# RWKV-6 attention and a SwiGLU feed-forward in one kernel: two casts of v go from ScalarE to VectorE, and products of r and k are placed behind the copies of x^T

## The chip, the core and the metric

The kernel runs on one core of one Trainium2 chip. A core has TensorE (PE) for matmuls, VectorE (DVE), ScalarE (ACT) and GpSimd (POOL) for everything elementwise, and SyncE (SP), which here only issues DMAs. Each engine works through its own queue in order, and semaphores tie the queues together. GpSimd issues the DMAs that cast weights from float32 to bfloat16 on their way, so those stand in its queue between its products. The metric is the device time of one execution in microseconds.

## What is computed

The reference has two parts. The first is a linear attention with a decaying state, for 4 batches, 8 heads, 768 steps and head size 48:

```
cur  = einsum('bhd,bhe->bhde', u * k[t], v[t])
y[t] = einsum('bhd,bhde->bhe', r[t], state + cur)
state = w[t][..., None] * state + einsum('bhd,bhe->bhde', k[t], v[t])
```

The second takes y as x, 3072 rows of 384, through an RMS norm with gain and a gated feed-forward (FFN) of width 1536:

```
xn  = x / sqrt(mean(x * x) + 1e-06) * rms_g
out = (silu(xn @ w_gate) * (xn @ w_val)) @ w_out
```

All inputs and the output are float32.

## The kernel before

**Tiles.** The 768 steps are cut into 6 superblocks of 128 steps. In a superblock the 4 batches give 4 units, so unit n.j is superblock n of batch j, a tile of 128 steps by 384 columns. A step of the program has a name such as k_mul.1.0: the function k_mul for unit 1.0. For the FFN the second number is one of 12 groups of 128 hidden columns, and the 512 rows of a whole superblock are worked at once.

**A unit's way.** load_r, load_k, load_v and load_w (lines 245 to 270) bring its inputs, issued by SP. ln, cs_mm, exp_r and exp_k make the decay factors. r_mul and k_mul (454 to 463) multiply r and k by them on VectorE and write the bfloat16 tile rk; from superblock 2 on, k_mul runs on GpSimd. rk_pe (480) transposes rk on TensorE, rk_tr (486) copies the result out of PSUM on ScalarE; from superblock 2 on a DMA transposes instead. q_mm (495) makes the products of all pairs of steps, q_mask_e and q_mask_o (508, 515) drop those of later steps; in superblock 0 both run on VectorE, later ScalarE copies the odd heads (q_copy_o) and GpSimd masks them. cast_v (376) makes a bfloat16 copy vb of v. y_mm (542) multiplies the masked products by vb and adds the old state's share; st_mm and st_new (523, 533) make the next state, also from vb. The step's own term, with u, goes over GpSimd: bonus_mul (465) is two products, bonus_sum (470) a sum by VectorE, bonus_v (475) a product with v; x_pe (in superblock 0) or x_add adds it. x_sq, x_rstd and xn_mul normalise, xn_pe (592) transposes x on TensorE and xn_out (598) copies x^T with the gain on VectorE.

**The FFN.** gate_mm and val_mm (637, 644) each do 3 matmuls on x^T of all 4 units, silu (651) runs on ScalarE, h_mul (655) on VectorE, and o_mm (668) does 12 matmuls per unit with wo_sb, then o_out and out_dma. The FFN of superblock n runs mixed with the attention of superblock n+1. load_gv.g.h (348) loads gate (h = 0) or value (h = 1) weights, piece 0 for groups 0 to 3 and piece 1 for groups 4 to 11; load_wo (356) loads w_out in three pieces of 4 groups. Both are issued from GpSimd's queue. The steps warm are matmuls on zeros, whose result is not used.

**What sets the order.** ORDER (line 25) is a list of all 1086 steps written out by hand, and the loop at line 691 calls them one after the other. Each engine gets its own steps in the order of the list. PSUM banks are handed out in the same order from three rings: a (2 banks: cs_r, gates, x_pe), b (2 banks: cs_k, values, x_pe) and q (4 banks: all else). A new step takes the bank whose last user comes earliest in the list, and waits for that user. Sets of units, such as CAST_ACT at line 177, choose the engine of a step.

The lines that the change touches in the code are these:

```
    CAST_ACT = sel("00 01 02 03 10 11 12 13")
...
        if (n, j) in CAST_ACT:
            nc.scalar.copy(out=vb[n, j], in_=inp["v", n, j])
        else:
            nc.gpsimd.tensor_copy(out=vb[n, j], in_=inp["v", n, j])
```

Of the kernel before, what the change touches and what calls it, by code (L numbers as in the profile page):

```python
# [41 lines left out]
xn_out.0.1 bonus_mul.1.1 warm.11.0 xn_mul.0.3 exp_k.1.3 xn_out.0.0 st_mm.0.3 xn_out.0.2 st_mm.0.2 xn_pe.0.3 exp_r.1.3
st_new.0.3 cs_mm.1.2 rk_pe.1.0 xn_out.0.3 k_mul.1.1 st_mm.0.1 st_new.0.1 k_mul.1.3 gate_mm.0.0 exp_r.1.2 bonus_sum.1.0
exp_k.1.2 rk_pe.1.1 gate_mm.0.3 rk_tr.1.0 val_mm.0.0 silu.0.0 bonus_sum.1.1 load_gv.1.1 load_r.2.2 bonus_mul.1.3
silu.0.3 val_mm.0.2 rk_tr.1.1 h_mul.0.0 gate_mm.0.2 st_new.0.2 silu.0.2 gate_mm.0.1 bonus_sum.1.3 val_mm.0.3
gate_mm.0.9 silu.0.1 h_mul.0.2 val_mm.0.1 gate_mm.0.6 silu.0.9 r_mul.1.3 h_mul.0.3 q_mm.1.0 h_mul.0.1 silu.0.6
q_mask_e.1.0 q_copy_o.1.0 q_mask_o.1.0 gate_mm.0.11 gate_mm.0.7 q_copy_o.1.1 silu.0.7 rk_pe.1.3 q_mask_e.1.1
q_mask_o.1.1 r_mul.1.2 bonus_v.1.0 val_mm.0.6 val_mm.0.7 cast_v.1.0 k_mul.1.2 rk_tr.1.3 gate_mm.0.5 h_mul.0.6 y_mm.1.0
load_wo.0.0 val_mm.0.9 silu.0.11 bonus_v.1.1 cast_v.1.2 load_wo.1.0 st_mm.1.0 cast_v.1.1 gate_mm.0.4 rk_pe.1.2
h_mul.0.7 st_mm.1.1 silu.0.5 val_mm.0.5 x_add.1.0 rk_tr.1.2 h_mul.0.9 cast_v.1.3 gate_mm.0.10 bonus_mul.1.2 val_mm.0.4  # L50
st_new.1.0 st_new.1.1 load_wo.2.0 q_mm.1.2 h_mul.0.5 silu.0.4 x_sq.1.0 h_mul.0.4 gate_mm.0.8 bonus_v.1.3 q_copy_o.1.3
x_rstd.1.0 q_mask_e.1.3 q_copy_o.1.2 val_mm.0.8 silu.0.8 val_mm.0.11 y_mm.1.1 silu.0.10 q_mask_e.1.2 bonus_sum.1.2
q_mask_o.1.3 h_mul.0.8 x_add.1.1 y_mm.1.3 st_mm.1.2 load_v.2.1 ln.2.0 st_mm.1.3 q_mask_o.1.2 val_mm.0.10 y_mm.1.2
x_sq.1.1 xn_mul.1.0 bonus_v.1.2 cs_mm.2.0 x_add.1.3 x_sq.1.3 st_new.1.2 h_mul.0.11 ln.2.1 h_mul.0.10 x_add.1.2
cs_add.2.0 o_mm.0.0 o_out.0.0 x_rstd.1.1 x_sq.1.2 xn_pe.1.0 xn_out.1.0 xn_mul.1.1 exp_r.2.0 st_new.1.3 cs_mm.2.1
cs_add.2.1 x_rstd.1.2 load_r.2.3 r_mul.2.0 o_mm.0.2 xn_pe.1.1 xn_mul.1.2 xn_pe.1.2 x_rstd.1.3 o_mm.0.1 xn_mul.1.3
bonus_mul.2.0 xn_out.1.1 exp_k.2.0 out_dma.0.0 load_k.2.2 exp_r.2.1 w_tot.2.0 load_v.2.0 ln.2.2 k_mul.2.0 ln.2.3
w_tot.2.1 r_mul.2.1 cs_mm.2.2 xn_pe.1.3 cs_mm.2.3 exp_k.2.1 xn_out.1.2 cs_add.2.2 k_mul.2.1 cs_add.2.3 cast_v.2.1
exp_r.2.2 exp_r.2.3 rk_tr.2.1 xn_out.1.3 o_mm.0.3 exp_k.2.3 o_out.0.1 w_tot.2.2 r_mul.2.2 bonus_mul.2.1 gate_mm.1.7
val_mm.1.7 exp_k.2.2 load_k.2.3 st_mm.2.1 rk_tr.2.0 bonus_sum.2.0 r_mul.2.3 w_tot.2.3 gate_mm.1.1 load_v.2.2 st_new.2.1  # L60
k_mul.2.2 silu.1.7 bonus_mul.2.2 silu.1.1 bonus_sum.2.1 val_mm.1.1 h_mul.1.7 gate_mm.1.6 silu.1.6 bonus_v.2.1
gate_mm.1.5 cast_v.2.0 k_mul.2.3 silu.1.5 rk_tr.2.2 val_mm.1.5 load_w.3.3 o_out.0.2 h_mul.1.1 gate_mm.1.3 gate_mm.1.0
val_mm.1.0 h_mul.1.5 o_out.0.3 silu.1.0 val_mm.1.6 q_mm.2.0 load_v.2.3 q_copy_o.2.0 silu.1.3 q_mask_o.2.0 gate_mm.1.2
st_mm.2.0 h_mul.1.0 val_mm.1.3 rk_tr.2.3 h_mul.1.6 load_w.3.1 load_w.3.0 gate_mm.1.10 val_mm.1.2 load_k.3.1
q_mask_e.2.1 silu.1.2 st_new.2.0 gate_mm.1.4 q_copy_o.2.1 cast_v.2.2 silu.1.4 q_mask_o.2.1 h_mul.1.3 q_mask_e.2.0
y_mm.2.1 y_mm.2.0 h_mul.1.2 st_mm.2.2 bonus_v.2.0 silu.1.10 x_add.2.1 x_add.2.0 gate_mm.1.9 val_mm.1.4 x_sq.2.1
gate_mm.1.8 val_mm.1.9 bonus_mul.2.3 st_new.2.2 out_dma.0.1 x_sq.2.0 h_mul.1.4 load_v.3.2 x_rstd.2.0 silu.1.9 silu.1.8
q_mm.2.2 bonus_sum.2.2 q_copy_o.2.2 h_mul.1.9 gate_mm.1.11 q_copy_o.2.3 out_dma.0.2 load_w.3.2 cast_v.2.3 bonus_v.2.2
bonus_sum.2.3 q_mask_o.2.3 st_mm.2.3 load_k.3.0 q_mask_o.2.2 q_mask_e.2.3 val_mm.1.11 q_mask_e.2.2 val_mm.1.10
bonus_v.2.3 y_mm.2.3 silu.1.11 y_mm.2.2 ln.3.0 h_mul.1.11 h_mul.1.10 x_rstd.2.1 x_add.2.2 ln.3.1 val_mm.1.8 ln.3.3  # L70
h_mul.1.8 cs_mm.3.0 load_r.3.0 x_sq.2.2 xn_mul.2.0 cast_v.3.2 cs_add.3.0 x_add.2.3 exp_k.3.0 x_sq.2.3 o_mm.1.0
cs_mm.3.1 xn_pe.2.0 exp_r.3.0 ln.3.2 x_rstd.2.2 o_mm.1.1 st_new.2.3 load_r.3.1 out_dma.0.3 w_tot.3.0 r_mul.3.0
xn_mul.2.1 k_mul.3.0 xn_mul.2.2 cs_add.3.1 exp_k.3.1 xn_pe.2.2 cs_mm.3.3 x_rstd.2.3 o_out.1.0 exp_r.3.1 bonus_mul.3.1
xn_out.2.2 xn_mul.2.3 o_mm.1.3 w_tot.3.1 xn_pe.2.3 o_out.1.1 cs_add.3.3 r_mul.3.1 load_k.3.2 load_r.3.3 xn_pe.2.1
xn_out.2.0 exp_r.3.3 exp_k.3.3 cs_mm.3.2 xn_out.2.3 o_mm.1.2 load_r.3.2 k_mul.3.1 w_tot.3.3 rk_tr.3.0 r_mul.3.3
cs_add.3.2 out_dma.1.0 xn_out.2.1 load_v.3.0 exp_r.3.2 gate_mm.2.5 exp_k.3.2 r_mul.3.2 w_tot.3.2 val_mm.2.0 gate_mm.2.0
bonus_mul.3.0 bonus_mul.3.2 k_mul.3.2 o_out.1.3 bonus_sum.3.0 silu.2.5 rk_tr.3.1 load_k.3.3 o_out.1.2 q_mm.3.0 silu.2.0
q_mask_e.3.0 val_mm.2.1 bonus_v.3.0 h_mul.2.0 gate_mm.2.1 load_w.4.1 load_v.3.1 load_k.4.3 st_mm.3.2 k_mul.3.3
q_copy_o.3.0 silu.2.1 rk_tr.3.2 load_v.4.0 rk_tr.3.3 val_mm.2.5 gate_mm.2.11 load_k.4.0 bonus_sum.3.1 cast_v.3.0
out_dma.1.1 load_v.3.3 load_w.5.2 q_mask_e.3.1 q_copy_o.3.1 gate_mm.2.2 silu.2.11 h_mul.2.5 val_mm.2.2 h_mul.2.1  # L80
load_w.4.0 gate_mm.2.3 load_v.4.1 silu.2.2 q_mask_o.3.0 cast_v.3.1 load_r.4.1 bonus_sum.3.2 h_mul.2.2 bonus_v.3.1
# [643 lines left out]
```

## Time and profile before

| what | value |
|---|---|
| three runs | 199.61, 200.89 and 200.95 us, median 200.89 |
| span of the profiled execution | 199.4 us |
| TensorE busy | 194.7 us |
| VectorE, ScalarE, GpSimd busy | 151.5, 137.1, 125.7 us |
| first matmul of the FFN (gate_mm.0.0) | 31.30 us from the span's start |
| first matmul with wo_sb (o_mm.0.0) | 52.66 us |

The profiled execution's own time is its span, first to last instruction. A timeline row reads: start, duration, engine, line, operation, output tile and input tiles, shape, count, and in brackets the idle time of that engine just before it with what ended it. Consecutive like instructions are merged, hence the count. In a row of waits stand the total, the number of times and the longest, in us. In a row of DMA issues stand the count, the size of one in KB as written, and the median time from the start of the issue to the landing. In a row for one line or tile stand the shortest, median and longest duration in ns, and the first and last start in us. Rows carry line numbers, not step names. The program's order gives the name: the n-th row of a line on an engine is the n-th step of that function in ORDER. The bank letters in ps_qu, ps_av and so on are the rings with one letter per bank (u, v, x, z).

### The profile page before, as it was taken

The numbers are of one execution on the slowest core, as the hardware profiler recorded it, in microseconds if no ns is written. First come the engines' busy times: TensorE is split into PE (matmuls) and PEld (weight loads), VectorE is DVE, ScalarE is ACT, GpSimd is POOL, SyncE is SP. The second block draws the span as 40 slices with busy tenths as digits, with TensorE's granted clock in tenths as the row PEclk, the third lists the DMA queues.
The fourth block names the chain that finished last, engine by engine and source line by source line (L and its number), as shares of the span: only waits on it lengthen the run. The fifth ranks groups of instructions, "written<-read, shape, count | busy, mean of one in ns | idle before, by whom it ended". The sixth has DMA issues, their size and how long they took to land.

```text
span 199.4 us, 4410 instructions
## 1 busy us (share of the span) xinstructions
PE 194.7 (98%) x1577; PEld 115.6 (58%) x1577; DVE 151.5 (76%) x290; ACT 137.1 (69%) x279; POOL 125.7 (63%) x184
## 2 busy tenths in 40 slices
...
GB/s 147 265 229 191 169 206 208 201 207 191 203 173 212 204 191 227 217 191 191 177 175 226 214 203 215 179 174 139 122 190 219 0 24 60 2 116 82 0 59 100
DMA packets 121566, 32.41 MB, mean 163 GB/s; under 512 B 116420, under 2 KB 120392, under 8 KB 121544
## 3 DMA queue, kind: packets, MB, share of 16 engines
...
q14 instruction: 10, 0.08, 0.1%
...
## 4 chain that ended last, share of the span: by engine, by line
PE 88%; DMA 5%; DVE 2%; POOL 2%; issue 1%; ACT 0%
PE ps_bu L626 12%; PE ps_av L626 12%; PE ps_au L626 11%; PE ps_bv L626 11%; PE ps_qu L672 7%; PE ps_qz L672 7%; DMA wg_sb<-in_moe_w_gate_dram 5%; PE ps_qx L672 5%; PE ps_qv L672 5%; PE ps_qz L502 1%; PE ps_qx L552 1%; PE ps_qv L502 1%; PE ps_qv L333 1%; PE ps_qu L285 1%; PE ps_qu L502 1%
## 5 line engine op out<-in xcount | busy, mean ns | idle before, releaser
L672 PEld LDWEIGHTS <-ht 128*128 128x128 bf16 x300 | 28.2, 98 | 16.6
L626 PEld LDWEIGHTS <-wg_sb 128*128 128x128 bf16 x216 | 23.1, 114 | 19.8 <-DMA wg_sb<-in_moe_w_gate_dram 0.9
L626 PEld LDWEIGHTS <-wv_sb 128*128 128x128 bf16 x216 | 23.0, 114 | 18.3
L658 DVE TENSOR_TENSOR ht<-ps_bv,sg 128x512 bf16<-128x512 f32 x35 | 24.0, 687 | 10.2 <-PE ps_bv L626 9.1
L658 DVE TENSOR_TENSOR ht<-ps_bu,sg 128x512 bf16<-128x512 f32 x37 | 25.4, 687 | 6.9 <-PE ps_bu L626 5.8
L235 ACT ACTIVATE sg<-ps_av 128x512 bf16<-128x512 f32 x37 | 22.0, 596 | 12.2 <-PE ps_av L626 11.6
L626 PE MATMUL ps_av<-xnt,wg_sb 128*128 128x512 bf16 x111 | 30.1, 380 | 0.0
L626 PE MATMUL ps_bu<-xnt,wv_sb 128*128 128x512 bf16 x111 | 30.1, 380 | 0.0
L626 PE MATMUL ps_au<-xnt,wg_sb 128*128 128x512 bf16 x105 | 28.5, 380 | 0.5 <-DMA wg_sb<-in_moe_w_gate_dram 0.5
L626 PE MATMUL ps_bv<-xnt,wv_sb 128*128 128x512 bf16 x105 | 28.5, 380 | 0.0
L235 ACT ACTIVATE sg<-ps_au 128x512 bf16<-128x512 f32 x35 | 21.0, 600 | 10.5 <-PE ps_au L626 8.7
L467 POOL TENSOR_TENSOR ruk<-rt,kt 128x384 f32<-128x384 f32 x24 | 24.0, 1001 | 6.1 <-DMA kt<-in_k_dram 5.2
L468 POOL TENSOR_TENSOR ruk<-ruk,u_bc 128x384 f32<-128x384 f32 x24 | 24.7, 1030 | 1.9
L520 POOL TENSOR_SCALAR_AFFINE_SELECT qts<-qts 128x512 bf16<-128x512 bf16 x20 | 12.8, 650 | 15.1 <-ACT qts L513 14.6
L477 POOL TENSOR_TENSOR ydiag<-vt,diag 128x384 f32<-128x384 f32 x24 | 20.2, 843 | 1.7 <-DVE diag L472 1.6
L461 POOL TENSOR_TENSOR rk<-kt,ek 128x384 bf16<-128x384 f32 x16 | 15.9, 1004 | 2.3 <-ACT ek L235 2.3
L672 PE MATMUL ps_qu<-wo_sb,ht 128*128 128x384 bf16 (+1 forms) x96 | 15.0, 306 | 0.0
L672 PE MATMUL ps_qz<-wo_sb,ht 128*128 128x384 bf16 x84 | 14.8, 326 | 0.0
L233 ACT ACT_TABLE_LOAD x10 | 12.8, 1283 | 1.8 <-PEq L709 1.6
L472 DVE TENSOR_REDUCE diag<-ruk 128x8 f32<-128x384 f32 x24 | 13.0, 543 | 0.2 <-POOL ruk L468 0.2
L235 ACT ACTIVATE lw<-wt 128x384 bf16<-128x384 f32 (+1 forms) x20 | 11.1, 577 | 2.6 <-DMA wt<-in_w_dram 2.6
L585 ACT ACTIVATE xn<-xb,rstd 128x384 bf16<-128x384 f32 x20 | 11.8, 603 | 0.8 <-POOL rstd L580 0.7
...
## 6 DMA issues: line engine op xcount, KB each, us to landing
rt<-in_r_dram SPq DMA_DIRECT2D x24, 192.0 KB, 4.0
kt<-in_k_dram SPq DMA_DIRECT2D x24, 192.0 KB, 4.2
vt<-in_v_dram SPq DMA_DIRECT2D x24, 192.0 KB, 4.0
out_dram<-ob SPq DMA_DIRECT2D x23, 192.0 KB, 2.3
wt<-in_w_dram SPq DMA_DIRECT2D x16, 192.0 KB, 4.0
wt<-in_w_dram SPq DMA_DIRECT2D x4, 384.0 KB, 4.4
wo_sb<-in_moe_w_out_dram POOLq DMA_DIRECT2D x3, 384.0 KB, 7.0
wg_sb<-in_moe_w_gate_dram POOLq DMA_DIRECT2D x1, 768.0 KB, 10.3
```

Source lines behind the costliest of these rows:

```text
L233: nc.scalar.preload_act_table_set(table_name)
L235: return nc.scalar.activation(**kw).ins
L461: eng.tensor_tensor(out=rk[:, n % 2, j, 1, :, 0:D], in0=inp["k", n, j], in1=bank["cs_k", n, j][:, 0:DM].rearrange("p (h d) -> p h d", h=H) ...
L467: nc.gpsimd.tensor_tensor(out=ruk[n, j], in0=inp["r", n, j], in1=inp["k", n, j], op=ALU.mult)
L468: nc.gpsimd.tensor_tensor(out=ruk[n, j], in0=ruk[n, j], in1=u_bc, op=ALU.mult)
L472: nc.vector.tensor_reduce(out=diag[n, j].rearrange("p h o -> p (h o)"), in_=ruk[n, j], axis=mybir.AxisListType.X, op=ALU.add)
L477: nc.gpsimd.tensor_tensor(out=ydiag[n, j], in0=inp["v", n, j], in1=diag[n, j].to_broadcast([128, H, D]), op=ALU.mult)
L520: nc.gpsimd.affine_select(out=qts[n, j][:, 1], in_=qts[n, j][:, 1], compare_op=ALU.is_gt, fill=0.0, base=0, pattern=[[0, NP], [1, 128]], c ...
L585: nc.scalar.activation(out=xn, in_=xb[n, j], func=AF.Copy, scale=rstd[n, j][:, 1, c:c + 1])
L626: nc.tensor.matmul(ps[:, cols], lhsT=units(ws, c, f), rhs=xnt[n][:, c, cols], start=(first and c == 0), stop=(c == KC - 1))
L658: nc.vector.tensor_tensor(out=ht[n][:, f, :], in0=bank.pop(("v", n, f)), in1=bank.pop(("sg", n, f)), op=ALU.mult)
L672: nc.tensor.matmul(ps[:, cols], lhsT=ht[n][:, f, b * L:(b + 1) * L], rhs=wo_sb[:, f, cols], start=(f == 0), stop=(f == FC - 1))
```

## The change

Two casts, those of units 0.2 and 0.3, go from ScalarE to VectorE:

```diff
-    CAST_ACT = sel("00 01 02 03 10 11 12 13")
+    CAST_ACT = sel("00 01 10 11 12 13")
+    CAST_DVE = sel("02 03")
...
         if (n, j) in CAST_ACT:
             nc.scalar.copy(out=vb[n, j], in_=inp["v", n, j])
+        elif (n, j) in CAST_DVE:
+            nc.vector.tensor_copy(out=vb[n, j], in_=inp["v", n, j])
         else:
```

In ORDER the same 1086 steps stand in another order. The diff of that list is mostly moved line breaks; sorted by engine it comes to this (a line with - is where a step stood, one with + where it stands now, and steps without a mark stay):

```
VectorE
   q_mask_e.0.0
 + bonus_sum.0.3
   q_mask_o.0.2
 - bonus_sum.0.3
   q_mask_e.0.2  q_mask_o.0.3
 + cast_v.0.2  cast_v.0.3
   q_mask_e.0.3
 - k_mul.1.0  r_mul.1.1  st_new.0.0  r_mul.1.0
 + r_mul.1.0  st_new.0.0
   xn_out.0.1  xn_out.0.0  xn_out.0.2
 - st_new.0.3  xn_out.0.3
 + xn_out.0.3  k_mul.1.0  r_mul.1.1  st_new.0.3
   k_mul.1.1  st_new.0.1
 - k_mul.1.3
   bonus_sum.1.0  bonus_sum.1.1  h_mul.0.0  st_new.0.2
 - bonus_sum.1.3
   h_mul.0.2  r_mul.1.3  h_mul.0.3  h_mul.0.1  q_mask_e.1.0  q_mask_e.1.1
 + k_mul.1.3
   r_mul.1.2  k_mul.1.2  h_mul.0.6
 + bonus_sum.1.3
   h_mul.0.7
...
 - r_mul.2.3  w_tot.2.3
 + w_tot.2.3  r_mul.2.3

ScalarE
   rk_tr.0.2  x_sq.0.1
 - cast_v.0.3
   rk_tr.0.3  x_rstd.0.1  exp_r.1.1
 - cast_v.0.2
   x_sq.0.0
...
   exp_r.1.2  exp_k.1.2
 + silu.0.0
   rk_tr.1.0
 - silu.0.0
   silu.0.3

GpSimd
   load_gv.0.0  bonus_v.0.2  bonus_v.0.3
 + load_gv.0.1
   bonus_mul.1.0
 - load_gv.0.1
   load_gv.1.0  bonus_mul.1.1  load_gv.1.1
 - bonus_mul.1.3
   q_mask_o.1.0
 + bonus_mul.1.3
   q_mask_o.1.1  bonus_v.1.0  load_wo.0.0

TensorE
   xn_pe.0.2  warm.11.0
 - st_mm.0.3  st_mm.0.2  xn_pe.0.3  cs_mm.1.2  rk_pe.1.0  st_mm.0.1
 + st_mm.0.2  xn_pe.0.3  st_mm.0.3  cs_mm.1.2  st_mm.0.1
 - gate_mm.0.0  rk_pe.1.1  gate_mm.0.3  val_mm.0.0
 + gate_mm.0.0  gate_mm.0.3  rk_pe.1.0  val_mm.0.0  rk_pe.1.1
   val_mm.0.2
...
   gate_mm.0.11  gate_mm.0.7
 - rk_pe.1.3
   val_mm.0.6  val_mm.0.7  gate_mm.0.5
 + rk_pe.1.3
   y_mm.1.0  val_mm.0.9  st_mm.1.0
 - gate_mm.0.4  rk_pe.1.2
 + rk_pe.1.2  gate_mm.0.4
   st_mm.1.1

SP
   load_v.1.0
 - load_v.1.1  load_v.1.2
 + load_v.1.2  load_v.1.1
   load_v.1.3
```

The banks of ring q that the moved steps get change names with the order, and so do those of later steps.

168 lines of the change are left out of this document (84 added, 84 removed).

## The prediction

> **What bounds the kernel now.** I read the page's busy times first, then what TensorE waited for, then the stretches of the trace in which the moved steps lie.
>
> ```profile
> PE 194.7 (98%) x1577; PEld 115.6 (58%) x1577; DVE 151.5 (76%) x290; ACT 137.1 (69%) x279; POOL 125.7 (63%) x184
> ```
> ```profile
> PE ps_au L626 <- DMA wg_sb<-in_moe_w_gate_dram: 0.5, 1, 0.5
> PE ps_qu L530 <- DVE xnt L607: 0.2, 1, 0.2
> ```
>
> TensorE is busy for 194.7 of the span's 199.4 us. Behind the kernel's first microseconds the list of its waits has only two entries: 0.5 us for a gate weight, and 0.2 us for a bank that the copy of x^T frees. After the gate weight it waits for nobody until the end. So a microsecond that TensorE gains or loses ahead of the last of these stays to the end, and what no queue brings to TensorE costs nothing. The change can at best remove what stands still here:
>
> ```profile
> 28.87 0.32 PE L374 MATMUL ps_qx<-still 128*128 128x384 bf16 x1
> 29.35 0.33 PE L530 MATMUL ps_qu<-vb,rk 128*128 128x96 bf16 x4 [0.16 <-DVE xnt L607]
> 29.52 0.33 PE L530 MATMUL ps_qx<-vb,rk 128*128 128x96 bf16 x4
> 29.82 0.33 PE L596 MATMUL ps_qv<-ident,xn 128*128 128x128 bf16 x3
> ...
> 34.99 0.81 PE L626 MATMUL ps_av<-xnt,wg_sb 128*128 128x512 bf16 x3
> 35.63 0.81 PE L626 MATMUL ps_bv<-xnt,wv_sb 128*128 128x512 bf16 x3
> 36.92 0.84 PE L626 MATMUL ps_au<-xnt,wg_sb 128*128 128x512 bf16 x3 [0.47 <-DMA wg_sb<-in_moe_w_gate_dram]
> ...
> 52.66 2.11 PE L672 MATMUL ps_qx<-wo_sb,ht 128*128 128x384 bf16 x12
> 54.60 0.33 PE L596 MATMUL ps_qv<-ident,xn 128*128 128x128 bf16 x3
> ```
>
> Durations overlap, so I go from start to start. One FFN group takes 0.64 us (34.99 to 35.63), but 35.63 to 36.92 is 1.29: gate_mm.0.9 loses **0.65 us**. Four st_mm matmuls take 0.17 (29.35 to 29.52); the two steps that wait for x^T take 0.48 and 0.30, so **0.44 us** is lost there. The sum, 1.1 us or 0.55% of the span, is nearly all that can be had.
>
> **What the change takes from VectorE and ScalarE ahead of x^T.** It moves bonus_sum.0.3 one step forward, puts two casts behind q_mask_o.0.3, and sends k_mul.1.0 and r_mul.1.1 behind the four xn_out.
>
> ```profile
> 23.24 0.69 DVE L517 TENSOR_TENSOR qts<-ps_qz,mask_lt 128x512 bf16<-128x512 f32 x1
> 23.85 0.68 DVE L509 TENSOR_TENSOR qts<-ps_qx,mask_lt 128x512 bf16<-128x512 f32 x1
> 24.45 0.55 DVE L461 TENSOR_TENSOR rk<-kt,ek 128x384 bf16<-128x384 f32 x1
> 24.91 1.35 DVE L455 TENSOR_TENSOR rk<-rt,er 128x384 bf16<-128x384 f32 x1
> 26.19 0.54 DVE L537 TENSOR_TENSOR st<-ps_qz,wcol 128x384 bf16<-128x384 f32 x1
> 26.66 2.18 DVE L455 TENSOR_TENSOR rk<-rt,er 128x384 bf16<-128x384 f32 x1
> ```
> ```profile
> L379 ACT CAST vb<-vt x8: 502/509/517, 16.7 to 46.7; 128x384 bf16<-128x384 f32 x8
> ```
> ```profile
> L679 DVE COPY ob<-ps_qz x2: 548/549/550, 84.9 to 120.3; 128x384 f32<-128x384 f32 x2
> ```
> ```profile
> 24.48 0.36 PE L552 MATMUL ps_av<-vb,qts 128*128 128x48 bf16 x8
> ```
>
> Ahead of the first xn_out VectorE drops k_mul.1.0 (0.46, start to start) and r_mul.1.1 (1.28), and gains two casts. No cast on VectorE is in the trace. The nearest rows are its copy of the same shape from PSUM, 0.55, and ScalarE's cast, 0.51; I take 0.5 each, 1.0 together, and bound one by 0.2 below and 1.35 above (the r_mul that shares its kind of memory). The Trainium skill, "VectorE: DVE Perf Modes", section "Mode 2×_2P — use both read ports for one tensor", lets such a copy take two elements per cycle; with the page's 0.96 GHz and about 150 cycles of start-up that is an estimate of (192 + 150)/0.96 = 0.36 us, which no run here shows yet, and by it the 0.3 charged below would go, the sum would be +0.5 and the time 201.4.
>
> So VectorE comes to xn_out.0.1 about 0.7 us sooner, and the 0.44 goes. ScalarE sheds two casts of 0.51; it then waits for TensorE's y_mm instead, so I count nothing more for it. In return y_mm.0.2, at 24.48, needs cast_v.0.2, which cannot start before q_mask_o.0.3 gives way at 23.85: done at 24.35 by my price, before 24.48, but 0.7 late at the upper bound. I charge 0.3 for that. k_mul.1.0 and r_mul.1.1 come due later, ahead of rk_pe.1.0 and rk_pe.1.1; those now stand behind two and three FFN groups of 0.64, which covers 1.3 to 1.9 us. silu.0.0 ahead of rk_tr.1.0, the rotated banks of st_mm, the swap of w_tot.2.3 with r_mul.2.3 and of load_v.1.1 with load_v.1.2 on SP have the same cover or touch only data that is there; I cost them at nothing, and without cover each costs at most one VectorE product, 0.5.
>
> **The weights' queue, GpSimd.** Its rows carry the forecast.
>
> ```profile
> 22.65 0.83 POOL L477 TENSOR_TENSOR ydiag<-vt,diag 128x384 f32<-128x384 f32 x1 [1.02 <-DVE diag L472]
> 23.44 0.99 POOL L467 TENSOR_TENSOR ruk<-rt,kt 128x384 f32<-128x384 f32 x1
> 24.51 1.34 POOL L468 TENSOR_TENSOR ruk<-ruk,u_bc 128x384 f32<-128x384 f32 x1
> 25.80 0.81 POOL L351 DMA_DIRECT2D wv_sb<-in_moe_w_val_dram  x1
> 26.60 0.77 POOL L351 DMA_DIRECT2D wg_sb<-in_moe_w_gate_dram  x1
> 27.40 1.01 POOL L467 TENSOR_TENSOR ruk<-rt,kt 128x384 f32<-128x384 f32 x1
> ...
> 30.46 1.01 POOL L467 TENSOR_TENSOR ruk<-rt,kt 128x384 f32<-128x384 f32 x1
> ...
> 40.23 1.54 POOL L520 TENSOR_SCALAR_AFFINE_SELECT qts<-qts 128x512 bf16<-128x512 bf16 x2 [7.48 <-ACT qts L513]
> ...
> 42.82 0.61 POOL L357 DMA_DIRECT2D wo_sb<-in_moe_w_out_dram  x1
> ...
> 44.85 1.01 POOL L467 TENSOR_TENSOR ruk<-rt,kt 128x384 f32<-128x384 f32 x1
> ...
> 46.88 0.59 POOL L357 DMA_DIRECT2D wo_sb<-in_moe_w_out_dram  x1
> ...
> 49.24 1.22 POOL L520 TENSOR_SCALAR_AFFINE_SELECT qts<-qts 128x512 bf16<-128x512 bf16 x2
> ```
> ```profile
> wg_sb<-in_moe_w_gate_dram POOLq DMA_DIRECT2D x1, 768.0 KB, 10.3
> ...
> wv_sb<-in_moe_w_val_dram POOLq DMA_DIRECT2D x1, 384.0 KB, 6.0
> ```
> ```profile
> wo_sb<-in_moe_w_out_dram POOLq DMA_DIRECT2D x1, 384.0 KB, 7.0
> ```
>
> *Front.* bonus_sum.0.3 moves ahead of one masking (0.61, from 23.24 to 23.85), so bonus_v.0.3 starts 0.6 sooner than 22.65. Behind it load_gv.0.1 now comes ahead of bonus_mul.1.0: its issue goes from 25.80 to about 22.85, and load_gv.1.0 from 26.60 to about 26.0. gate_mm.0.9 waits for the latter, which landed at 26.60 + 10.3 = 36.9. It lands at least 0.6 sooner, and more if the 384 KB ahead of it, 6.0 from issue to landing, are done when it starts. TensorE is there at 36.28 less 0.44 plus 0.3, 36.1. So the 0.65 goes: 36.1 against 36.92 is **0.8 us gained** (0.3 to 1.1).
>
> *Back.* bonus_mul.1.3 ran at 30.46, ahead of 7.48 us in which GpSimd waited for q_copy_o.1.0. Now it stands behind q_mask_o.1.0, on the queue that then issues wo_sb. Such a pair takes 2.03 (44.85 to 46.88). q_copy_o comes 0.8 sooner with TensorE, and the two maskings, 1.54 with a wait between them where 1.22 is clean, give back 0.3. So bonus_v.1.0, the three wo_sb issues and all behind them start 2.03 - 0.8 - 0.3 = **0.9 us later**.
>
> Is that covered? The third piece of wo_sb is issued at 46.88 and lands 7.0 later, at 53.9. o_mm.0.0 has 12 matmuls from 52.66 to 54.60, 0.162 each; its ninth, the first to read that piece, starts at 52.66 + 8 x 0.162 = 53.95. The cover is 0.1 us. So the ninth matmul goes to 53.95 + 0.9 - 0.1 = 54.75, **0.8 us later than now**, even though TensorE arrives 0.8 earlier. The 0.8 won at the front turns into a wait of 1.6. q_mask_o.1.3 is late by the same 0.9, but y_mm.1.3 would wait ahead of the same o_mm, and the two don't add.
>
> VectorE keeps o_mm.0.0 from running ahead as well:
>
> ```profile
> 53.45 0.68 DVE L658 TENSOR_TENSOR ht<-ps_bu,sg 128x512 bf16<-128x512 f32 x1
> ```
>
> This is h_mul.0.10, done at 54.13; the eleventh matmul, at 54.28, reads it. k_mul.1.3 and bonus_sum.1.3 (0.5 each) come behind q_mask_e.1.1 and h_mul.0.6 in the changed order, so VectorE has 1.0 more to do between there and h_mul.0.10 and starts it at most 1.1 sooner: a tie again.
>
> **The sum.** Gate weight and x^T: -1.1; cast ahead of y_mm.0.2: +0.3; new wait at o_mm.0.0: +1.6. Together +0.8 us, from 199.4 to 200.2 in the profiled execution's own terms. The three runs have 199.61, 200.89 and 200.95; the span is 0.2 under the lowest and 1.5 under the median. On the median, 200.89 + 0.8 = **201.7 us**.
>
> **Rivals.**
>
> *A, the gain holds.* The wo_sb pieces may follow each other in one queue and need less than 7.0 once the gate and value weights are out of the way sooner, or q_copy_o may come early enough. Against it: GpSimd has to make up 2.03, and TensorE offers at most 1.1 plus 0.3. If wo_sb lands on time and VectorE follows, 0.1 to 1.1 are gained; at 0.8, 200.1.
>
> *B, GpSimd and VectorE stop each other.*
>
> ```profile
> L455 DVE TENSOR_TENSOR rk<-rt,er x2: 1352/1764/2176, 24.9 to 26.7; 128x384 bf16<-128x384 f32 x2
> ...
> L455 DVE TENSOR_TENSOR rk<-rt,ps_av x1: 547/547/547, 19.7 to 19.7; 128x384 bf16<-128x384 f32 x1
> ```
>
> With one operand in PSUM r_mul takes 0.55; with both in SBUF it took 1.35 and 2.18. Each time it ended 0.4 after the GpSimd product that it ran into: 24.91 + 1.35 = 26.26 against 24.51 + 1.34 = 25.85, and 26.66 + 2.18 = 28.84 against 27.40 + 1.01 = 28.41. In the changed order both casts meet bonus_mul.1.0, and k_mul.1.3, r_mul.1.2 and k_mul.1.2 meet bonus_mul.1.3. Then the casts cost up to 0.85 more each, which holds y_mm.0.2 and y_mm.0.3, and three products 0.4 to 0.8 more each, which holds h_mul.0.10. It decides once VectorE is over 1.1 late there: 1.2 beyond the forecast, 202.9. The Trainium skill, "GPSIMD Engine Reference", section "8. Key points", says that GpSimd shares its SBUF interfaces with VectorE and contends with VectorE instructions in a 2-port mode or with two SBUF inputs. The two rows of r_mul agree; by that rule the casts would be slowed too, which no run here shows yet.
>
> *C, it does nothing.* If the waits at the front only change owner and wo_sb ties as before, the time stays within 0.1 of 200.9. The exact tie at o_mm.0.0 speaks for it, the 2.03 against it.
>
> *D, a starved load.*
>
> ```profile
> kt<-in_k_dram SPq DMA_DIRECT2D x1, 192.0 KB, 14.4
> ```
>
> This is load_k.1.2, issued at 26.27 among the weights: SP's loads crawl while the weights run. With load_gv.0.1 2.95 sooner, r and k of units 1.1 and 1.3 fall into that stretch. load_k.1.1 also gates bonus_mul.1.1 and behind it load_gv.1.1, which val_mm.0.6 reads. If load_r.1.3 lands only behind the weights, r_mul.1.3 holds VectorE and h_mul.0.10 by about 1.5: 202.4.
>
> **How the numbers follow.** The forecast's mechanism (wo_sb late, 0.1 to 1.4 slower) has 0.50, A 0.25, B 0.10, D 0.07, C 0.08. A's far end gives 200.89 - 1.1 = 199.8; B gives 202.9. The range 199.7 to 202.9 holds A, C, D and the forecast and most of B. The forecast's own range is 201.0 to 202.3. Over 1% is 2.0 us, about what a measurement of this kernel can tell from no change. To gain that, more than the 1.1 us that stands still would have to go: 0.03. To lose it takes B beyond its point, or B and the forecast's upper end: 0.09. Within 1%: 0.88.
>
> **What would show it.** Right: gate_mm.0.9 starts near 36.1 without a wait; load_gv.0.1 is issued near 22.9; the first wo_sb issue is near 43.7 and the third near 47.8; TensorE has a new wait of 1 to 2 us ended by the DMA of wo_sb within o_mm.0.0, and no other behind it. Wrong: o_mm.0.0 ends before 54.6 (A); a wait for qts or ht ends last there (B or D); the casts on VectorE take over 0.8; gate_mm.0.9 still waits.

## The result and the profile after

The change makes the kernel a little slower, by 0.8% in one comparison and 0.4% in another. In the first comparison the changed kernel has a median of 202.23 us (6 runs, 202.10 to 202.41) and the kernel before 200.49 us (6 runs, 199.61 to 200.95): ratio 1.0084 [1.0062, 1.0107]. A second comparison on another chip, told below, has 12 runs of the changed kernel (median 202.30) against 29 of before (median 201.51) and gives 1.0039 [1.0012, 1.0065]. In microseconds that is 1.2 to 2.1 and 0.2 to 1.3. Ratios leave out slow runs, those more than 1.5% above the fastest of their kernel. The changed kernel's median hardly differs between the two comparisons, before's does; why it does isn't known. The two profiled spans differ by 1.0: 199.4 before, 200.4 after (that execution took 202.1 us). The granted TensorE clock was 1.0 in both.

The page's busy times of the changed kernel:

```profile
PE 191.2 (95%) x1557; PEld 114.1 (57%) x1577; DVE 151.6 (76%) x292; ACT 136.5 (68%) x277; POOL 125.1 (62%) x184
```

The two casts are there (VectorE 290 to 292 instructions, ScalarE 279 to 277). TensorE's 191.2 is no gain: 20 of its 1577 matmul records are missing from this trace. Its waits say more; the columns are bank, line, releaser, then total, count and longest in us:

```profile
PE ps_au L405 <- ACT lw L236: 1.2, 1, 1.2
PE ps_qu L286 <- DVE half_of L296: 1.0, 1, 1.0
PE ps_qu L675 <- DMA wo_sb<-in_moe_w_out_dram: 0.7, 1, 0.7
PE ps_av L555 <- DVE vb L382: 0.6, 1, 0.6
PE ps_bv L629 <- DVE ht L661: 0.5, 1, 0.5
PE ps_qv L375 <- ACT rkT L496: 0.4, 1, 0.4
PE ps_qu L555 <- POOL qts L523: 0.3, 1, 0.3
PE ps_qz L487 <- DVE rk L458: 0.2, 1, 0.2
```

The lines are those of the changed kernel: 1 higher than before's up to line 378, 3 higher behind it. The two waits of the prediction's view, wg_sb and the bank behind the x^T copy, are gone. The rows for lw, half_of, rkT and rk lie in the first 20 us, where executions differ by 2 us anyway (below). New are four: vb (the casts), ht, qts, and at last wo_sb. TensorE's timeline of the changed kernel shows where they stand:

```profile
24.40 0.36 PE L555 MATMUL ps_av<-vb,qts 128*128 128x48 bf16 x8 [0.56 <-DVE vb L382]
...
35.09 0.81 PE L629 MATMUL ps_bv<-xnt,wv_sb 128*128 128x512 bf16 x3
35.74 0.81 PE L629 MATMUL ps_au<-xnt,wg_sb 128*128 128x512 bf16 x3
...
42.21 0.33 PE L552 MATMUL ps_qx<-st,rkT 128*128 128x96 bf16 x4
...
43.28 0.81 PE L629 MATMUL ps_bv<-xnt,wv_sb 128*128 128x512 bf16 x3 [0.54 <-DVE ht L661]
...
50.97 0.35 PE L555 MATMUL ps_qu<-vb,qts 128*128 128x48 bf16 x7 [0.32 <-POOL qts L523]
...
52.78 1.46 PE L675 MATMUL ps_qu<-wo_sb,ht 128*128 128x384 bf16 x8
54.97 0.81 PE L675 MATMUL ps_qu<-wo_sb,ht 128*128 128x384 bf16 x4 [0.73 <-DMA wo_sb<-in_moe_w_out_dram]
55.62 0.33 PE L599 MATMUL ps_qv<-ident,xn 128*128 128x128 bf16 x3
```

gate_mm.0.9 (35.74) follows one group of 0.65 behind val_mm.0.3 and is 1.18 us earlier than before's 36.92. y_mm.1.0, at 42.21, is still 1.04 earlier than 43.25 before. Then three waits give it back, one after the other. I take each from start to start against the same stretch of before, of which these are y_mm.1.0, val_mm.0.9 and val_mm.0.10:

```profile
43.25 0.33 PE L549 MATMUL ps_qz<-st,rkT 128*128 128x96 bf16 x4
...
43.62 0.82 PE L626 MATMUL ps_bv<-xnt,wv_sb 128*128 128x512 bf16 x3
...
51.36 0.81 PE L626 MATMUL ps_bu<-xnt,wv_sb 128*128 128x512 bf16 x3
```

In the changed kernel val_mm.0.9 comes at 43.28 for 43.62, so the lead is 0.34. The wait for qts within y_mm.1.3 takes the rest: val_mm.0.10 comes at 51.49 for 51.36. In o_mm.0.0 the first eight matmuls run, and the other four wait for the third piece of wo_sb. xn_pe.1.0, the row behind o_mm.0.0, starts at 55.62 for 54.60: 1.02 late. Behind it nothing changes any more: o_mm.5.4 starts at 196.28 for 195.27.

What holds TensorE is read on GpSimd's timeline:

```profile
23.38 0.81 POOL L352 DMA_DIRECT2D wv_sb<-in_moe_w_val_dram  x1
...
39.04 0.63 POOL L523 TENSOR_SCALAR_AFFINE_SELECT qts<-qts 128x512 bf16<-128x512 bf16 x1 [9.15 <-ACT qts L516]
39.65 1.30 POOL L470 TENSOR_TENSOR ruk<-rt,kt 128x384 f32<-128x384 f32 x1
41.02 1.19 POOL L471 TENSOR_TENSOR ruk<-ruk,u_bc 128x384 f32<-128x384 f32 x1
42.17 0.95 POOL L523 TENSOR_SCALAR_AFFINE_SELECT qts<-qts 128x512 bf16<-128x512 bf16 x1
...
43.87 0.61 POOL L358 DMA_DIRECT2D wo_sb<-in_moe_w_out_dram  x1
...
47.93 0.59 POOL L358 DMA_DIRECT2D wo_sb<-in_moe_w_out_dram  x1
...
50.29 1.22 POOL L523 TENSOR_SCALAR_AFFINE_SELECT qts<-qts 128x512 bf16<-128x512 bf16 x2
```

load_gv.0.1 is issued at 23.38 for 25.80; 22.9 was forecast. bonus_mul.1.3 runs from 39.65 to 42.21, between the two maskings. Its two products take 2.52 from start to start, where such a pair took 2.03 before. The first wo_sb issue is at 43.87 for 42.82, the third at 47.93 for 46.88, and q_mask_o.1.3 at 50.29 for 49.24: all 1.05 late. The third piece lands at 54.93, 7.0 behind its issue as before, and the four matmuls start at 54.97.

VectorE at the same time, and its two casts at the front:

```profile
23.15 2.29 DVE L382 CAST vb<-vt 128x384 bf16<-128x384 f32 x2
...
39.42 0.66 DVE L464 TENSOR_TENSOR rk<-kt,ek 128x384 bf16<-128x384 f32 x1
40.01 1.35 DVE L458 TENSOR_TENSOR rk<-rt,er 128x384 bf16<-128x384 f32 x1
41.28 1.35 DVE L464 TENSOR_TENSOR rk<-kt,ek 128x384 bf16<-128x384 f32 x1
42.55 0.68 DVE L661 TENSOR_TENSOR ht<-ps_bv,sg 128x512 bf16<-128x512 f32 x1
```

r_mul.1.2 and k_mul.1.2 (40.01 and 41.28) run beside bonus_mul.1.3 and take 1.35 each. Before they took 0.66 and 0.98:

```profile
40.62 0.66 DVE L455 TENSOR_TENSOR rk<-rt,er 128x384 bf16<-128x384 f32 x1
41.20 0.98 DVE L461 TENSOR_TENSOR rk<-kt,ek 128x384 bf16<-128x384 f32 x1
```

k_mul.1.3, the row at 39.42, now also stands ahead of them and takes 0.59 from start to start. So h_mul.0.6, the row at 42.55, is 0.32 later than before's 42.23 although TensorE is 1.0 ahead, and val_mm.0.9 waits for it. About 0.6 of VectorE's delay is the moved k_mul.1.3, the other 0.9 the two slower products.

### The profile page after: what moved, and what is told of

Same layout as the page of the kernel before. It is cut to its first block, busy times and chain, and to the rows that moved or that the text cites. A ratio compares the mean times of both kernels' runs of the same rounds, so it can differ in the third digit from the quotient of the medians.

```text
span 200.4 us, 4388 instructions
## 1 busy us (share of the span) xinstructions
PE 191.2 (95%) x1557; PEld 114.1 (57%) x1577; DVE 151.6 (76%) x292; ACT 136.5 (68%) x277; POOL 125.1 (62%) x184
## 4 chain that ended last, share of the span: by engine, by line
PE 71%; POOL 8%; issue 7%; SPq 6%; DMA 6%; ACT 0%; POOLq 0%
PE ps_av L629 10%; PE ps_bu L629 10%; PE ps_bv L629 9%; PE ps_au L629 9%; PE ps_qz L675 7%; PE ps_qx L675 7%; PE ps_qv L675 5%; PE ps_qu L675 4%; SPq L249 4%; DMA wo_sb<-in_moe_w_out_dram 3%; POOL ruk L470 3%; DMA rt<-in_r_dram 2%; SPq L262 2%; POOL ruk L471 2%; POOL ydiag L480 1%
## 5 line engine op out<-in xcount | busy, mean ns | idle before, releaser
L675 PEld LDWEIGHTS <-ht 128*128 128x128 bf16 x300 | 28.2, 98 | 17.5 <-issue 1.0
L629 PEld LDWEIGHTS <-wv_sb 128*128 128x128 bf16 x216 | 22.9, 114 | 18.9 <-issue 0.6
L629 PE MATMUL ps_bu<-xnt,wv_sb 128*128 128x512 bf16 x103 | 29.3, 380 | 0.4
L471 POOL TENSOR_TENSOR ruk<-ruk,u_bc 128x384 f32<-128x384 f32 x24 | 24.2, 1008 | 1.9
L675 PE MATMUL ps_qz<-wo_sb,ht 128*128 128x384 bf16 (+1 forms) x96 | 15.0, 306 | 0.0
L675 PE MATMUL ps_qx<-wo_sb,ht 128*128 128x384 bf16 x84 | 14.8, 326 | 0.0
L573 ACT ACTIVATE junk<-xb 128x384 bf16<-128x384 f32 x20 | 10.4, 522 | 2.8 <-DVE xb L564 2.6
```

Of the source, the lines that this page charges most:

```text
L471: nc.gpsimd.tensor_tensor(out=ruk[n, j], in0=ruk[n, j], in1=u_bc, op=ALU.mult)
L573: nc.scalar.activation(out=junk, in_=xb[n, j], func=AF.Square, accum_out=rstd[n, j][:, 0, c:c + 1])
L629: nc.tensor.matmul(ps[:, cols], lhsT=units(ws, c, f), rhs=xnt[n][:, c, cols], start=(first and c == 0), stop=(c == KC - 1))
L675: nc.tensor.matmul(ps[:, cols], lhsT=ht[n][:, f, b * L:(b + 1) * L], rhs=wo_sb[:, f, cols], start=(f == 0), stop=(f == FC - 1))
```

## Experiments

The theory: the loss is the place of bonus_mul.1.3 on GpSimd's queue, ahead of the w_out issues. The rivals: the casts beside GpSimd's work carry it, or VectorE's products do, or some transfer that starts elsewhere. Each kernel changes places in ORDER or the engine of a cast. Its ratio is to runs of before on the same chip: e1 to e4 share one chip, e5 to e8 a second, e9 to e11 a third.

| kernel | ratio [95%] | span | o_mm.0.0 done |
|---|---|---|---|
| before / after, first profiles | | 199.4 / 200.4 | 54.60 / 55.62 |
| e1: after, bonus_mul.1.3 back | 0.9985 [0.9956, 1.0014] | 199.5 | 54.78 |
| e2: after, w_out issues sooner | 1.0045 [1.0022, 1.0068] | 200.4 | 55.64 |
| e3: after, casts back | 1.0054 [1.0030, 1.0078] | 200.4 | 55.66 |
| e4: before, bonus_mul.1.3 late | 1.0050 [1.0028, 1.0073] | 200.3 | 55.57 |
| e5: after, unit 1.3 back | 1.0013 [0.9976, 1.0049] | 199.8 | 54.89 |
| e6: before again | 0.9983 [0.9953, 1.0013] | 199.0 | 54.00 |
| e7: before, casts on VectorE | 1.0014 [0.9987, 1.0042] | 200.3 | 55.47 |
| e8: e5, weights sooner | 0.9992 [0.9959, 1.0025] | 200.0 | 55.04 |
| e9: front only, w_out sooner | 1.0020 [0.9993, 1.0047] | 199.4 | 54.62 |
| e10: after again | 1.0039 [1.0012, 1.0065] | 200.6 | 55.78 |
| e11: front only | 1.0002 [0.9969, 1.0036] | 198.9 | 54.12 |

"Done" is the start of the step behind it, xn_pe.1.0. From there to the last matmuls every trace has the same length within 0.3 us, so this column is where the profiles part. It comes from one execution each, and the spans of before's runs beside e1 to e4 go from 198.5 to 201.3 us. The column therefore shows where time goes in a profile; whether two kernels differ is for the ratio to say.

### Bonus_mul.1.3 back in its place (e1)

```diff
-q_copy_o.1.0 q_mask_o.1.0 bonus_mul.1.3 gate_mm.0.11
+q_copy_o.1.0 q_mask_o.1.0 gate_mm.0.11
-load_gv.1.1 load_r.2.2 silu.0.3
+load_gv.1.1 bonus_mul.1.3 load_r.2.2 silu.0.3
```

> The changed kernel with one step put back: bonus_mul.1.3 stands right behind load_gv.1.1 again, ahead of q_mask_o.1.0. Theory (the change loses its front gain because bonus_mul.1.3 delays GpSimd's w_out issues and locks VectorE's products around 40 us): the first w_out issue comes near 41.5 instead of 43.87, no wait for the w_out DMA in o_mm.0.0, r_mul.1.2 and k_mul.1.2 take 0.55 instead of 1.35 and the 0.5 wait for h_mul.0.6 goes; o_mm.0.0 ends 1.5 to 2 us sooner; 200.2 to 200.7, 1.5 to 2 us under the changed kernel. Rival (the loss is at the front, in the casts on VectorE): 202.2, unchanged. Rival (r and k of unit 1.3 land late): GpSimd waits for them and the queue is as late as in the changed kernel.

The loss is gone: 0.9985 [0.9956, 1.0014]. On GpSimd's timeline the w_out issues stand 1.0 sooner than in the changed kernel, even though bonus_v.1.0 waits for v:

```profile
41.95 0.94 POOL L480 TENSOR_TENSOR ydiag<-vt,diag 128x384 f32<-128x384 f32 x1 [0.63 <-DMA vt<-in_v_dram]
42.84 0.61 POOL L358 DMA_DIRECT2D wo_sb<-in_moe_w_out_dram  x1
...
46.94 0.59 POOL L358 DMA_DIRECT2D wo_sb<-in_moe_w_out_dram  x1
```

TensorE then goes through all twelve matmuls of o_mm.0.0 without a wait:

```profile
52.83 2.11 PE L675 MATMUL ps_qu<-wo_sb,ht 128*128 128x384 bf16 x12
54.78 0.33 PE L599 MATMUL ps_qv<-ident,xn 128*128 128x128 bf16 x3
```

VectorE's two products are free of it too:

```profile
40.75 0.98 DVE L458 TENSOR_TENSOR rk<-rt,er 128x384 bf16<-128x384 f32 x1
41.65 0.54 DVE L464 TENSOR_TENSOR rk<-kt,ek 128x384 bf16<-128x384 f32 x1
```

With that one step back all three late waits (ht, qts, wo_sb) are gone. It is not the whole story, since the 1.1 us that the front should have won isn't there either: 54.78, not 53.5, and 0.84 us sooner than in the changed kernel instead of the 1.5 to 2 expected. The first w_out issue came at 42.84, not near 41.5, and r_mul.1.2 still took 0.98.

### The same step alone, in the kernel before (e4)

```diff
-bonus_mul.1.3 silu.0.3 val_mm.0.2
+silu.0.3 val_mm.0.2
-q_mask_o.1.0 gate_mm.0.11
+q_mask_o.1.0 bonus_mul.1.3 gate_mm.0.11
```

bonus_sum.1.3, which reads its result, moves behind h_mul.0.6.

> The kernel before with bonus_mul.1.3 behind q_mask_o.1.0 and, because it waits for it, bonus_sum.1.3 behind h_mul.0.6; nothing else changed. Theory: GpSimd issues w_out 1.7 us later (2.03 less 0.3), o_mm.0.0 waits for it by about 1.6: 1.3 to 1.9 us over the kernel before, 201.8 to 202.4, that is as slow as the changed kernel without its front gain being there. Rival (the delay of GpSimd's queue is hidden, the front decides): 200.5.

TensorE's timeline of this kernel has the waits for qts and wo_sb again:

```profile
51.22 0.35 PE L552 MATMUL ps_qx<-vb,qts 128*128 128x48 bf16 x7 [0.65 <-POOL qts L520]
...
54.92 0.81 PE L672 MATMUL ps_qx<-wo_sb,ht 128*128 128x384 bf16 x4 [0.42 <-DMA wo_sb<-in_moe_w_out_dram]
```

The ratio, 1.0050 [1.0028, 1.0073], is like that of the whole change. So the step, with the sum that waits for it, is enough to make the loss, and by e1 it is needed for it. The wait for ht (0.5 in the changed kernel) isn't in this list: k_mul.1.3 stands in its old place here, so bonus_mul.1.3 alone doesn't make that wait. The time lost is 0.8 us by the medians and 0.6 to 1.5 by the interval, where 1.3 to 1.9 was expected; the span, 200.3, is within 0.1 of the changed kernel's.

### The casts back on ScalarE (e3)

```diff
-    CAST_ACT = sel("00 01 10 11 12 13")
-    CAST_DVE = sel("02 03")
+    CAST_ACT = sel("00 01 02 03 10 11 12 13")
+    CAST_DVE = sel("")
```

cast_v.0.3 and cast_v.0.2 also go back to their old places in ORDER.

> The changed kernel with the two casts back on ScalarE in their old places. Theory: the wait of 0.6 for cast_v.0.2 ahead of y_mm.0.2 goes, TensorE and q_copy_o.1.0 come 0.3 to 0.7 sooner, GpSimd's queue is sooner by the same, and so is the wait for w_out: 0.3 to 0.7 under the changed kernel, 201.5 to 201.9. Rival (all of the loss comes from the casts): 200.5 or less. Rival (ScalarE's two casts hold x_sq instead): 202.2.

No gain, where 0.3 to 0.7 us was expected: 1.0054 [1.0030, 1.0078]. y_mm.0.2 starts at 23.70 for 24.40, 0.7 sooner. But TensorE then waits at the next gate:

```profile
35.89 0.84 PE L629 MATMUL ps_au<-xnt,wg_sb 128*128 128x512 bf16 x3 [0.68 <-DMA wg_sb<-in_moe_w_gate_dram]
```

gate_mm.0.9 is at 35.89 for 35.74, and o_mm.0.0 ends as late as in the changed kernel (55.66 for 55.62). What the casts cost ahead of gate_mm.0.9 is covered by the weight's arrival there.

### The w_out issues ahead of the products (e2)

```diff
-bonus_sum.1.3 y_mm.1.0 load_wo.0.0 val_mm.0.9 silu.0.11 bonus_v.1.1 cast_v.1.2 load_wo.1.0 st_mm.1.0
+bonus_sum.1.3 y_mm.1.0 val_mm.0.9 silu.0.11 bonus_v.1.1 load_wo.2.0 cast_v.1.2 st_mm.1.0
-q_mask_o.1.1 r_mul.1.2
+q_mask_o.1.1 load_wo.0.0 load_wo.1.0 r_mul.1.2
```

> The changed kernel with the three w_out issues moved forward within GpSimd's queue: the first two right behind q_mask_o.1.1, the third ahead of bonus_mul.1.2. Theory (three waits give the gain back one after the other, and the last one, for w_out, is 0.8): that wait goes or shrinks to 0.1, the waits for h_mul.0.6 (0.5) and for q_mask_o.1.3 stay, now some 0.1 to 0.2 later; 0.6 to 0.9 us under the changed kernel, 201.3 to 201.6. Rival (only the w_out load counts and the others are hidden behind it): 1.5 to 2 us under it. Rival (w_out earlier starves the loads of v): slower than 202.2.

Not as expected: the weight comes sooner (its third piece lands at 53.1) and the view of TensorE's waits no longer has wo_sb, but the time stays at 1.0045 [1.0022, 1.0068]. bonus_v.1.0 now stands behind two issues, and VectorE waits for it at x_add.1.0; then TensorE waits for VectorE. VectorE's row, and TensorE's:

```profile
45.33 0.56 DVE L564 TENSOR_TENSOR xb<-ps_qx,ydiag 128x384 f32<-128x384 f32 x1 [0.83 <-POOL ydiag L480]
```
```profile
48.67 0.23 PE L507 MATMUL ps_qz<-rkT 48*128 48x128 bf16 x1 [0.61 <-DVE st L540]
```

With bonus_mul.1.3 in that place, giving the issues precedence only changed who waits.

### Unit 1.3 back, and the kernel before again (e5, e6)

e5 puts bonus_mul.1.3, k_mul.1.3 and bonus_sum.1.3 back; casts, front order and the swap of the v loads stay.

```diff
-q_mask_e.1.1 k_mul.1.3 q_mask_o.1.1
+q_mask_e.1.1 q_mask_o.1.1
-h_mul.0.6 bonus_sum.1.3 y_mm.1.0
+h_mul.0.6 y_mm.1.0
-q_mask_o.1.0 bonus_mul.1.3 gate_mm.0.11
+q_mask_o.1.0 gate_mm.0.11
-st_new.0.1 gate_mm.0.0
+st_new.0.1 k_mul.1.3 gate_mm.0.0
-load_gv.1.1 load_r.2.2
+load_gv.1.1 bonus_mul.1.3 load_r.2.2
-gate_mm.0.1 val_mm.0.3
+gate_mm.0.1 bonus_sum.1.3 val_mm.0.3
```

> The changed kernel with all three late steps of unit 1.3 back: bonus_mul.1.3 behind load_gv.1.1, k_mul.1.3 behind st_new.0.1, bonus_sum.1.3 behind h_mul.0.0 and st_new.0.2. Theory (o_mm.0.0 is a tie of three: TensorE, the third w_out piece, VectorE's h_mul.0.10; with bonus_mul.1.3 back only VectorE is late): h_mul.0.10 ends about 1 us sooner than in e1, 52.7 to 53.3 instead of 54.3, o_mm.0.0 ends at 53.9 to 54.4, span 198.7 to 199.2; 0.3 to 0.7 us under e1 and under the kernel before. Rival (w_out holds the tie alone): like e1, span 199.5.

Not as expected: the ratio is 1.0013 [0.9976, 1.0049], and h_mul.0.10 ends at 54.12 instead of 52.7 to 53.3. GpSimd, no longer late, waits for v instead. Its timeline:

```profile
42.05 0.83 POOL L480 TENSOR_TENSOR ydiag<-vt,diag 128x384 f32<-128x384 f32 x1 [1.54 <-DMA vt<-in_v_dram]
...
44.38 0.82 POOL L480 TENSOR_TENSOR ydiag<-vt,diag 128x384 f32<-128x384 f32 x1 [0.96 <-DMA vt<-in_v_dram]
...
47.81 0.59 POOL L358 DMA_DIRECT2D wo_sb<-in_moe_w_out_dram  x1
```

The second row is bonus_v.1.1 waiting for the load that the change put behind load_v.1.2; it was issued at 40.37 and took 3.9 to land. So the third w_out piece is issued at 47.81, only 0.12 sooner than in the changed kernel. In the changed kernel bonus_mul.1.3 hides this wait: bonus_v.1.1 starts at 44.50 there without one.

> The kernel before, unchanged, for a second profile. In the first one cs_mm.0.3 started at 16.06, in five others at 13.95 to 14.74, though nothing ahead of it is changed. Theory: the start varies from run to run and is swallowed by later waits, here by the gate weight (gate_mm.0.9 near 36 to 37) and by o_mm.0.0, which ends within 0.4 us of the first profile's 54.60; span 198.9 to 199.5. Rival (the front's lead reaches the end in the kernel before): o_mm.0.0 ends at 53 to 53.5, span 197.9 to 198.4.

The kernel before, profiled again, ends 0.4 us sooner (span 199.0) and shows a larger wait for the gate weight. TensorE's timeline:

```profile
36.17 0.84 PE L626 MATMUL ps_au<-xnt,wg_sb 128*128 128x512 bf16 x3 [1.19 <-DMA wg_sb<-in_moe_w_gate_dram]
...
54.00 0.33 PE L596 MATMUL ps_qv<-ident,xn 128*128 128x128 bf16 x3
```

This matters for reading the first profile. There cs_mm.0.3 started at 16.06; here it starts at 14.10, and in the changed kernel at 14.25. TensorE reached the FFN 1.45 us later in that execution (gate_mm.0.0 at 31.30 for 29.85), so the wait for wg_sb came out short, and the wait for x^T, which e6's list doesn't have, was there. Against a like start the change is 0.43 us sooner at gate_mm.0.9 (35.74 for 36.17), not 1.18, and 1.62 later behind o_mm.0.0 (55.62 for 54.00). GpSimd's maskings and its first and third w_out issue in e6:

```profile
39.49 1.54 POOL L520 TENSOR_SCALAR_AFFINE_SELECT qts<-qts 128x512 bf16<-128x512 bf16 x2 [6.93 <-ACT qts L513]
...
42.52 0.61 POOL L357 DMA_DIRECT2D wo_sb<-in_moe_w_out_dram  x1
...
46.57 0.59 POOL L357 DMA_DIRECT2D wo_sb<-in_moe_w_out_dram  x1
```

Against these the changed kernel's issues (43.87 and 47.93) are 1.35 and 1.36 late, not 1.05. e6's end, 0.6 ahead of the first profile's 54.60, lies outside the 0.4 that I had expected; its gate_mm.0.9 and its span lie inside.

### The casts alone (e7)

```diff
-bonus_sum.0.3 q_mask_e.0.2
+cast_v.0.2 cast_v.0.3 bonus_sum.0.3 q_mask_e.0.2
```

The two steps leave their old places, and run on VectorE in the kernel before.

> The kernel before with the two casts on VectorE and nothing else, both put ahead of bonus_sum.0.3, so that GpSimd, which waits for that sum, has nothing to do during the second. In the changed kernel each took 1.17 to 1.19 us beside bonus_mul.1.0. Theory (GpSimd and VectorE stop each other there): the second cast takes 0.3 to 0.55 here and ends when it likes; the time is that of the kernel before within 0.4 us, since the 0.7 to 1.0 us that bonus_v.0.3 is later is taken up by the wait for the gate weight or adds to it. Rival (the cast itself is that slow on VectorE): 1.1 or more each here as well.

In the profile the casts cost 1.0 each and TensorE waits 1.4 for qts from the masking behind them. The casts' row:

```profile
L382 DVE CAST vb<-vt x2: 1005/1012/1020, 21.4 to 22.3; 128x384 bf16<-128x384 f32 x2
```

The row has the shortest, median and longest cast in ns. GpSimd wasn't idle at that place as I had expected, so e7 doesn't tell a held cast from a slow one; e1's shortest cast, 0.35 (below), does. The first cast (from 21.40) ends 0.18 behind the issue of load_gv.0.0 (21.25 to 22.24), the second (from 22.35) 0.23 behind bonus_v.0.2 (22.28 to 23.12). The profiled execution ends late, at 55.47, but the runs don't show that the kernel is slower: 1.0014 [0.9987, 1.0042].

### The weights further ahead (e8)

e5, and load_gv.1.0 goes ahead of bonus_mul.1.0, the second w_out issue right behind the first, the third behind bonus_v.1.1.

```diff
-bonus_v.0.3 load_gv.0.1 warm.20.0
+bonus_v.0.3 load_gv.0.1 load_gv.1.0 warm.20.0
-y_mm.1.0 load_wo.0.0 val_mm.0.9 silu.0.11 bonus_v.1.1 cast_v.1.2 load_wo.1.0 st_mm.1.0
+y_mm.1.0 load_wo.0.0 load_wo.1.0 val_mm.0.9 silu.0.11 bonus_v.1.1 load_wo.2.0 cast_v.1.2 st_mm.1.0
```

> e5 with the weights moved forward in GpSimd's queue: load_gv.1.0 right behind load_gv.0.1 and ahead of bonus_mul.1.0, the second w_out issue right behind the first and the third ahead of bonus_mul.1.2. Theory: gate_mm.0.9 has no wait, the third w_out piece lands near 52, the tie at o_mm.0.0 is left to TensorE and VectorE; o_mm.0.0 ends at 53.2 to 54.0, span 198.0 to 198.8, 1 to 1.5 us under the kernel before. Rival (more weights in front starve r and k of units 1.1 to 1.3 and v of superblock 1): VectorE waits near 30 or ScalarE's casts near 42, no gain over e5 or slower.

No gain: 0.9992 [0.9959, 1.0025], o_mm.0.0 done at 55.04. load_gv.1.0 landed at 34.7, before TensorE asked for it, and the third w_out piece at 53.6. But load_k.1.3 came at 34.0 for 28.2 to 32.0 in the others, and VectorE, which needs it, was late in turn; TensorE's list has a wait of 0.9 us for ht, the output of h_mul.

### The front order alone, with w_out sooner and without (e9, e11), and the change again (e10)

e11 keeps of the change mainly the order at the front: products of units 1.0 and 1.1 behind x^T, their transposes behind FFN groups, load_gv.0.1 sooner. The moved places of rk_pe.1.2 and rk_pe.1.3, of silu.0.0 and of w_tot.2.3 stay too. The three steps of unit 1.3, the casts and the loads of v are as before. e9 is e11 with each w_out issue at least one product further ahead.

```diff
-load_v.1.0 load_v.1.2 load_v.1.1
+load_v.1.0 load_v.1.1 load_v.1.2
-q_mask_o.1.1 r_mul.1.2 bonus_v.1.0 val_mm.0.6
+q_mask_o.1.1 load_wo.0.0 r_mul.1.2 bonus_v.1.0 load_wo.1.0 val_mm.0.6
-bonus_v.1.1 cast_v.1.2 load_wo.1.0
+bonus_v.1.1 load_wo.2.0 cast_v.1.2
```

The first pair of lines is in both, the others in e9 alone.

> Only what helped of the change, and w_out moved forward: load_gv.0.1 ahead of bonus_mul.1.0 and the products behind x^T as in the changed kernel; the casts back on ScalarE, unit 1.3's three steps back, load_v.1.1 ahead of load_v.1.2 again; w_out's issues one step ahead of bonus_v.1.0, bonus_v.1.1 and bonus_mul.1.2. Theory: GpSimd waited 0.6 to 1.5 for v of unit 1.0 ahead of the first w_out issue, that issue now uses this wait and comes near 41 instead of 42.8, the third piece lands near 52 to 53, the tie at o_mm.0.0 is left to TensorE and VectorE; o_mm.0.0 ends at 53.2 to 53.9, span 198.2 to 198.9; 0.1 to 0.8 us under the kernel before. Rival (what comes in by DMA up to 54 us sets the end, in whatever order): 54.0 to 54.6, span 199.0 to 199.6, no difference.

> e9 without the w_out moves: the change without the casts, without the late steps of unit 1.3 and without the swap of load_v. Theory: gate_mm.0.9 comes 0.2 to 0.5 sooner than in the kernel before, bonus_v.1.1 does not wait for v of unit 1.1, the w_out issues are at most as late as before, and o_mm.0.0 ends within 0.3 us of the kernel before's 54.0 to 54.6: span 198.8 to 199.5, no difference that can be measured, since w_out and v come in when the DMA traffic lets them. Rival (the front gain of 0.8 is worth 0.8 once GpSimd is not late): span 198.2 or less.

> The changed kernel again, beside the others on one chip. Theory: o_mm.0.0 ends at 55.3 to 55.9 whatever the start was like, span 200.2 to 200.6, 1.0 to 1.7 us over the kernel before. Rival (0.84% was a chance of the chip): within 0.5 us of the kernel before.

e10 repeats the loss, and its o_mm.0.0 and span fall where expected, but by the medians it is 0.8 us over before, not 1.0 to 1.7 (1.0039 [1.0012, 1.0065]). The last wait is the same, 0.5 us for wo_sb in o_mm.0.0.

e9 and e11 have no wait for a weight at all. e9's third w_out piece lands at 52.4, far ahead of need; behind the first microseconds TensorE's list is empty. Yet o_mm.0.0 is done at 54.62 in e9, where 53.2 to 53.9 was expected, and at 54.12 in e11, as expected. e9 began like the first profile of before (cs_mm.0.3 at 16.18), which ended at 54.60; e11 began like e6 (14.12), which ended at 54.00. So against like starts no gain of the front order shows, and the ratios show none (1.0020 [0.9993, 1.0047] and 1.0002 [0.9969, 1.0036]). e11's list shows part of why:

```profile
PE ps_qv L487 <- DVE rk L464: 0.4, 1, 0.4
```

This is rk_pe.1.1, waiting for k_mul.1.1. VectorE's r_mul.1.1, behind x^T, ran 1.87 beside GpSimd's work (29.68 to 31.55), and k_mul.1.1 0.88 beside bonus_mul.1.3. The gain at gate_mm.0.9 (35.97 for 36.17) is 0.2, at val_mm.0.9 it is gone (42.87 for 42.88). In e9 the last 0.26 goes between val_mm.0.9 (43.36 for 43.62) and val_mm.0.5 (45.73 for 45.72), in slivers that no row names. What holds TensorE there wasn't isolated.

## Why the prediction was right, and where not

**The time and the range.** The forecast was 201.7 us, 0.8 over the median of three runs, with a range of its own of 201.0 to 202.3. The measured 202.23 lies in it, near its upper end. It is 1.7 over before's median of six in the first comparison, twice the forecast change, and 0.8 over in the second.

**The step that decides was right; its size was partly luck.** bonus_mul.1.3 behind q_mask_o.1.0 was said to make the w_out issues 0.9 late, and o_mm.0.0 with them. Forecast and measured: first issue 43.7 and 43.87; third 47.8 and 47.93; ninth matmul 54.75 and 54.97. e1 takes the step away and the loss goes; e4 adds it with its sum and the loss comes. The 0.9 was 2.03 for the pair, less 0.8 for an earlier q_copy_o, less 0.3. The pair took 2.52 beside VectorE's products, 0.5 more: B named what the two engines cost VectorE, nobody named what it costs GpSimd. q_mask_o.1.0 came 1.19 sooner (39.04 for 40.23), 0.4 more. The two misses nearly cancel, and the 1.19 is owed to the slow start of the first profile: against e6's 39.49 it is 0.45. Against that start the issues are 1.35 late, and TensorE is 1.62 late behind o_mm.0.0.

**The new wait was 0.7 us by the profile, 0.9 from start to start, not 1.6.** "A new wait of 1 to 2 us" thus failed as a sign. The third piece landed 0.2 later than forecast, and TensorE came much later than I said. The forecast counted the wait for qts as one that "doesn't add", and VectorE as a tie. Both came first and used up the lead: 0.70 at val_mm.0.9 and 0.47 at y_mm.1.3 (from 0.34 ahead to 0.13 behind). The end is nearly the same, because the last wait sets it. "No other behind it" holds, but a single new wait it was not.

**Rival B happened as well.** r_mul.1.2 and k_mul.1.2 took 1.35 each beside bonus_mul.1.3, 0.7 and 0.4 more than before and so within the 0.4 to 0.8 per product which B named; its third product, k_mul.1.3, took only 0.66. B's deciding point of 1.1 wasn't reached: h_mul.0.10 was at 53.56 for 53.45. The Trainium skill, "GPSIMD Engine Reference", section "8. Key points", says that GpSimd contends with VectorE instructions that have two SBUF inputs or run in a 2-port mode. The rows agree for the products (0.98 and 0.54 in e1, 1.35 and 1.35 in the changed kernel).

**The casts cost twice what was charged.** 0.5 each was the price, 0.3 the charge ahead of y_mm.0.2. In the changed kernel they took 1.20 and 1.18, over the 0.8 that was named as a sign of being wrong, and y_mm.0.2 waited 0.56 for the first. Two kernels with the same order at that place show how wide it goes. Rows of the groups by line in e1 and e10, shortest, median, longest in ns:

```profile
L382 DVE CAST vb<-vt x2: 346/435/524, 23.8 to 24.2; 128x384 bf16<-128x384 f32 x2
```
```profile
L382 DVE CAST vb<-vt x2: 524/1191/1858, 23.5 to 23.9; 128x384 bf16<-128x384 f32 x2
```

The same cast takes 0.35 in one execution and 1.86 in another, each time as the second of the two. The upper bound of 1.35 was too low, and one price for both was wrong. The Trainium skill, "VectorE: DVE Perf Modes", section "Mode 2×_2P — use both read ports for one tensor", led to the estimate 0.36, and the shortest casts agree (346 ns in e1). The miss didn't show in the time: e3 has the casts back and loses as much.

**The front gain of 1.1 was mostly that one execution's.** The 0.65 at the gate weight and 0.44 at x^T were read from a profile whose first 16 us were 2 us slow. In e6, without that delay, nothing is lost at x^T, more stands still at the gate weight (1.19), and the change takes 0.43 of it. In e9 and e11 no gain is left at o_mm.0.0. So rival A fell too: no kernel here shows a gain clear of noise, not even those without the late w_out. The sum came out near because the landing of w_out set the end, and the front gain enters that landing only through q_copy_o.

**The swap of the v loads, costed at nothing, was nothing only while GpSimd was late.** e5 shows bonus_v.1.1 waiting 0.96 for it. This is a cover that should have been named. Rival D's wait for a starved load wasn't seen in the changed kernel: load_k.1.3 landed at 29.5 for 28.2 before, and bonus_mul.1.3 came long behind it. e8, which pushes the weights further ahead, shows such a wait (k.1.3 2 to 6 us later than in the others). Rival C is ruled out by both comparisons, whose intervals lie above 1.

**Span and time.** The forecast added 0.8 to the median of three runs, 200.89, which gave 201.7. In the later profiles the time is 1.7 to 1.8 above the span, so 199.4 stands for 201.1 and the forecast span for 201.9; the changed kernel's 200.4 went with 202.1. The profiled execution of before was thus slower than each of its six timed runs (199.61 to 200.95), which is why the spans differ by 1.0 where the medians differ by 1.7.
